# A scan kernel regrouped: from 128 tokens of one sequence per tile to 64 tokens of each of two sequences

## The chip, the cores and the metric

One core of one Trainium2 chip. The metric is device microseconds (us) of one execution; lower is better. The engines named below are PE (TensorE: matrix products; PEld is its weight load), DVE (VectorE), ACT (ScalarE), POOL (GpSimd, used here mostly to issue DMAs, those that add into their destination among them) and SP (SyncE, used only to issue DMAs).

## The reference

Two blocks, one after the other. The first is a gated linear recurrence per batch entry b (4) and head h (8), with 768 steps and a head size of 48:

```
scale = min(|a|, 0.999) / (|a| + 1e-6);   a = (a_re + i a_im) * scale
S_t   = diag(a_t) S_{t-1} + k_t v_t^T            (complex S, 48 x 48, real k and v)
y_t   = q_t^T Re(S_t)
```

The outputs y are laid out as 3072 tokens x 384 features (batch and step, head and head dimension), and the second block is a maxout network on them:

```
h   = max(x w1, x w2, x w3)        (384 -> 768)
out = h w_out                      (768 -> 384)
```

All inputs are float32 except the four weight matrices, which arrive as float64.

## The kernel before, in words

**Tiles and groups.** A tile x is 128 tokens of one sequence (all heads and features, 384 columns); a group g is the two tiles, x = 2g and x = 2g + 1 (written x and y in the schedule's words), of a pair of sequences. There are 12 groups: six steps of 128 tokens for sequences 0 and 1, then six for sequences 2 and 3 (`NS` = 6). Within a tile the recurrence is worked in two chunks of 64 tokens. A complex decay is a magnitude and an angle; products of decays become sums of logarithms and sums of angles.

**The steps of a group.** `gates` (L501) makes the logarithm of the magnitude (tile `Ln`) and the angle in turns (tile `w`) for both tiles at once. `angles` (L582) sums the angles over tokens: step `cs` multiplies a triangle of ones, `upto`, by `w` on PE; `t` (ACT) and `nf` (DVE) take off whole turns; `Cd` sends the last token's sum to the first token of the next group's angles, by a DMA of POOL's that adds into the tile `ar` of group g + 1. There it is added after step `half` (DVE) has made `ar` and before step `turn` (DVE) reads it. `turns` (L618) sums `Ln` by matrix products `sums` and `F`, takes exponentials on ACT, and multiplies k and q by them and by sine and cosine (`mk`, `mq`, `uk`, `uq`, `kEn` on DVE); `tp` transposes on PE, and `Kc` and `Qc` copy to SBUF on ACT or DVE. `factors` (L683) makes the scaled copies `Q1`, `Q2`, `KB`, `QB`, `QG` on DVE. `scores` (L714) makes the masked 64 x 64 score blocks from `A` and `B`.

**The state.** `state` (L766) keeps the states that a tile's two chunks start from in the buffers `g0` to `g3`. `dk` (PE) is the sum of k v^T of a chunk; `h0` to `h3` (L784) move the state on: `h0` multiplies by the first chunk's decay and `h1` adds its `dk`, which gives the state for the second chunk; `h2` and `h3` do the same for the second chunk, which gives the state for the next tile of the sequence. Each works on all heads of one chunk (384 elements a partition), on DVE, and on ACT where there is only `dk` to copy. The first step of a pair of sequences starts from zero, and the last one leaves out `h2`, `h3` and half of `dk`.

**Outputs.** `outputs` (L801), step `y`, adds the score product and, where there is a state, the product of `QG` with the state. The maxout block takes a group's 256 tokens at a time: `U` (PE, three weight blocks of 128 columns at a time) and `u` (the maximum), and for the second product seven half-size products `P1` to `P7` with sums `S1` to `S4`. Group 0 is done tile by tile with tiles xT and hT instead, while the weights are still being turned from float64 to float32 by steps `Wa` to `Wg` on ACT, DVE and POOL.

**What sets the order.** Nothing is scheduled at run time. `SCHEDULE` (L21) is a written list of words `step:group`; `run` (L954) issues each word's instructions, and `Bound` (L199) ties each engine to the order of issue, so every engine (and each DMA queue, SP's and POOL's) works through its own instructions strictly in that order. `SLOTS` (L124) names which of four pairs of PSUM banks each product uses. A word in `OTHER` (L131) goes to the second of two places: a load to POOL's queue and not SP's, a copy, an absolute value or a maximum to DVE and not ACT, an addition to DVE and not to a DMA of POOL's.

The products of `cs` are these: for each chunk and each half of the heads the weights are 128 tokens x 64, so that a chunk's sums run over all tokens of the tile up to its own.

```python
for ch in range(2):
    for j in range(2):
        dst, m = ps[j * L64:(j + 1) * L64, ch * HC:(ch + 1) * HC], slice(ch * L64, (ch + 1) * L64)
        mm(out=dst, lhsT=upto[:, m], rhs=every(T["w", g][:, c * DM:(c + 1) * DM], j), start=True, stop=True)
```

Of the kernel before, what the change touches and what calls it, by code (L numbers as in the profile page):

```python
# [26 lines left out]
mqx:0 Wa10:0 nfx:0 WL11:0 afx:0 csy:0 Wb10:0 ty:0 sqr:1 Wc9:0 Wc10:0 T2:0 nfy:0 sbx:0 sax:0 We9:0 ukx:0 Wf9:0 f1x:0
t2:0 f2x:0 We10:0 Lix:2 uqx:0 Lky:0 f2y:0 tpkx:0 kEnx:0 Wf10:0 f0x:0 sqi:1 Wa11:0 WL1:0 Wb11:0 add:1 sumsy:0 Eky:0
tpqx:0 CL:0 Qcx:0 Kcx:0 Wa1:0 Q2x:0 lnL:1 WL2:0 Q1x:0 Eqy:0 relu:1 Wb1:0 Wc11:0 T1:0 expe:1 Eny:0 Wc1:0 expw:1 abs:1
Lvx:0 Lry:2 t1:0 We11:0 dkx:0 h1x:0 xor:1 Ax:0 Wf11:0 Wa2:0 Lqy:0 lne:1 g0x:0 We1:0 Liy:2 g1x:0 Lkx:1 Wb2:0 QBx:0  # L30
half:1 g2x:0 Wc2:0 g3x:0 pw:1 Wf1:0 M0:0 afy:0 lnw:1 h2x:0 WL4:0 Lnop:1 expL:1 We2:0 Wa4:0 KBx:0 mulai:1 mulw:1 h3x:0
Cdy:0 Wb4:0 Bx:0 stt:1 Lrx:2 sqr:2 Wf2:0 say:0 sby:0 QGx:0 M1:0 b1x:0 atan:1 mqy:0 Wc4:0 uqy:0 Wg1:0 b0x:0 yx:0 Cdx:0
tpqy:0 sqi:2 add:2 xor:2 turn:1 lnL:2 Lvy:0 relu:2 Lqx:1 WL5:0 We4:0 xx:0 Qcy:0 mky:0 M2:0 Wf4:0 expe:2 Wa5:0 csx:1
uky:0 m0:0 m1:0 Q2y:0 Lqy:1 tpky:0 Fx:1 tx:1 Kcy:0 f0x:1 Q1y:0 nfx:1 csy:1 QBy:0 Ay:0 expw:2 Wg2:0 abs:2 kEny:0 Wg4:0
Wb5:0 WL7:0 U01x:0 ty:1 g0y:0 f1x:1 lne:2 nfy:1 dky:0 g1y:0 f2x:1 f3x:1 addw:2 Wa7:0 half:2 Cdx:1 u01x:0 U11x:0 Z2:0
g2y:0 Wc5:0 g3y:0 KBy:0 h1y:0 By:0 b1y:0 b0y:0 QGy:0 lnw:2 Cdy:1 We5:0 Wb7:0 Wf5:0 sumsx:1 h2y:0 u11x:0 expL:2 mulai:2
yy:0 xy:0 mulw:2 Eqx:1 Wc7:0 Ekx:1 Enx:1 U02x:0 h3y:0 afx:1 sax:1 stt:2 Wg5:0 afy:1 We7:0 U02y:0 U01y:0 U11y:0 WL8:0
u02x:0 atan:2 U12y:0 turn:2 sbx:1 Wf7:0 u01y:0 u02y:0 Lix:4 u11y:0 Fy:1 Wg7:0 sumsy:1 Wa8:0 Wb8:0 mkx:1 u12y:0 mqx:1
U21y:0 sby:1 f0y:1 Wc8:0 csx:2 Lnop:2 f1y:1 f3y:1 Lkx:2 f2y:1 Z4:0 Eky:1 csy:2 Eny:1 u21y:0 Eqy:1 uqx:1 ty:2 tpqx:1
Qcx:1 U21x:0 We8:0 ukx:1 tpkx:1 u21x:0 Lvx:2 Wf8:0 nfy:2 Kcx:1 tx:2 Z3:0 Wg8:0 Lky:1 kEnx:1 sumsx:2 nfx:2 Fx:2 U22y:0  # L40
h0x:1 u22y:0 Lvx:1 QBx:1 say:1 Lqy:2 dkx:1 Liy:3 mqy:1 Q1x:1 Enx:2 Q2x:1 mky:1 afx:2 sax:2 Lvy:2 KBx:1 h1x:1 sbx:2
h2x:1 Ekx:2 Eqx:2 uqy:1 afy:2 Oy:0 oy:0 Liy:4 tpqy:1 h3x:1 uky:1 QGx:1 Bx:1 Qcy:1 Ax:1 tpky:1 f1x:2 f0x:2 f2x:2 f3x:2
Q1y:1 Kcy:1 Lqx:2 g0x:1 Q2y:1 sby:2 say:2 U22x:0 g1x:1 g2x:1 g3x:1 mkx:2 Lrx:3 u22x:0 Lix:3 KBy:1 Lvy:1 sqi:3 b1x:1
Ay:1 sumsy:2 kEny:1 mqx:2 Lky:2 QBy:1 uqx:2 b0x:1 Eky:2 U12x:0 u12x:0 Eqy:2 yx:1 xx:1 ukx:2 Lry:3 tpqx:2 tpkx:2 Eny:2
g0y:1 Qcx:2 g1y:1 g2y:1 g3y:1 sqr:3 xor:3 add:3 lnL:3 relu:3 h0y:1 dky:1 By:1 Q1x:2 QGy:1 h1y:1 J3:0 h2y:1 Dy:0 Kcx:2
Q2x:2 Ox:0 b1y:1 mqy:2 b0y:1 ox:0 yy:1 mky:2 uky:2 xy:1 QGx:2 expe:3 Lqx:3 Ax:2 g0x:2 Lrx:4 expw:3 abs:3 half:3 addw:3
# [5 lines left out]
P4:1 h3y:2 expw:4 r1:1 abs:4 addw:4 g1y:2 g2y:2 lne:4 P6:1 xor:4 sax:3 QGy:2 g3y:2 Px:1 sby:3 P7:1 sbx:3 Dx:0 P3:1
mqx:3 r6:1 half:4 h0x:3 P2:1 By:2 r5:1 r7:1 r57:1 oy:1 lnw:4 sumsy:3 b1y:2 b0y:2 Fy:3 ukx:3 Cdx:3 Eny:3 uqx:3 Eky:3
expL:4 ox:1 Cdy:3 Eqy:3 f3y:3 Lvy:3 f0y:3 yy:2 xy:2 tpqx:3 mulai:4 tpkx:3 Qcx:3 mqy:3 Lnop:4 mulw:4 QBx:3 Q1x:3 Lky:3
say:3 stt:4 sqi:5 uqy:3 Lry:5 sqr:5 Kcx:3 KBx:3 mky:3 U01:2 Lvx:3 Q2x:3 U02:2 f2y:3 uky:3 add:5 f1y:3 Dx:1 u01:2 u02:2
# [87 lines left out]
def kernel(  # L143
# [15 lines left out]
    P = 128  # L159
# [882 lines left out]
```

## Time and profile before

| what | value |
|---|---|
| three runs | 566.14, 567.57, 568.57 us; median 567.57 |
| the profiled execution | 566.42 us, its span 564.7 us |
| mean granted TensorE clock | 0.978 |
| PE, DVE, ACT, POOL busy | 527.8, 490.0, 391.5, 153.5 us |
| HBM read, written | 33.03 MB, 4.72 MB |
| POOL's DMAs of step `Cd` (ar<-nf) | 40, median 3.1 us from issue to landing |

The page gives the busy time of each engine, the span in 40 equal slices of 14.1 us (a digit is the busy share in tenths; PEclk is the granted clock), the chain that ended last and the costliest groups of instructions. A busy time is the union of the instructions' intervals. Consecutive instructions of one engine overlap a little in these records, so the distance from one start to the next is shorter than a mean duration. The code is issued through one helper, so all work carries line L208, and the rows are told apart by their tiles (`out<-in`). Each float32 matrix product shows as two records.

### The profile page before, as it was taken

The numbers are of one execution on the slowest core, as the hardware profiler recorded it, in microseconds if no ns is written. First come the engines' busy times: TensorE is split into PE (matmuls) and PEld (weight loads), VectorE is DVE, ScalarE is ACT, GpSimd is POOL, SyncE is SP. The second block draws the span as 40 slices with busy tenths as digits, with TensorE's granted clock in tenths as the row PEclk, the third lists the DMA queues.
The fourth block names the chain that finished last, engine by engine and source line by source line (L and its number), as shares of the span: only waits on it lengthen the run. The fifth ranks groups of instructions, "written<-read, shape, count | busy, mean of one in ns | idle before, by whom it ended". The sixth has DMA issues, their size and how long they took to land.

```text
span 564.7 us, 22778 instructions
## 1 busy us (share of the span) xinstructions
PE 527.8 (93%) x10086; PEld 452.2 (80%) x10086; DVE 490.0 (87%) x777; ACT 391.5 (69%) x668; POOL 153.5 (27%) x243
## 2 busy tenths in 40 slices
PE   2568799999998999999999999999999999999997
PEld 1345597678887888988888888998888898988896
DVE  7999959999998999999999889999998868997324
ACT  7898868976888878998686897766668644641100
POOL 8615553304040030102605205215550181000000
PEclk9779989999999999999999999999999999999999
DMA  9995983514424244717307323525341132000000
GB/s 249 267 253 88 193 171 68 104 33 81 78 47 89 53 87 87 141 35 139 59 11 156 58 42 68 99 46 110 76 90 28 30 60 73 3 30 2 2 29 28
DMA packets 108916, 47.53 MB, mean 84 GB/s; under 512 B 95633, under 2 KB 100241, under 8 KB 108817
## 3 DMA queue, kind: packets, MB, share of 16 engines
q1 hardware_dynamic: 99136, 31.08, 24.9%
q0 software_dynamic: 9680, 14.99, 14.3%
q8 instruction: 79, 1.29, 0.9%
q14 instruction: 21, 0.16, 0.1%
HBM read 33.03 MB, written 4.72 MB: 67 GB/s over the span
## 4 chain that ended last, share of the span: by engine, by line
PE 75%; ACT 6%; DVE 2%; issue 1%; SPq 1%; DMA 1%; DVEq 0%; ACTq 0%
PE up L208 30%; PE op L208 21%; PE y L208 6%; PE A L208 4%; PE tp L208 4%; PE dk L208 3%; PE sums L208 2%; PE cs L208 2%; ACT L208 2%; PE F L208 1%; PE B L208 1%; SPq L208 1%; DMA ar<-in_a_re_dram 1%; DVE atm L208 1%; ACT f L208 1%
## 5 line engine op out<-in xcount | busy, mean ns | idle before, releaser
L208 PE MATMUL up<-xhx,w 128*128 128x256 f32 x792 | 177.7, 382 | 0.7 <-ACT K L208 0.4
L208 PEld LDWEIGHTS up<-xhx,w 128*128 128x128 f32 x792 | 148.4, 190 | 22.5 <-ACT K L208 0.6
L208 ACT ACT_TABLE_LOAD x59 | 75.7, 1283 | 1.7 <-PEq L1026 0.8
L208 POOL DMA_DIRECT2D ar<-nf x40 | 35.7, 1261 | 73.9 <-DVE ar L208 71.1
L208 PE MATMUL op<-wo,xhx 128*128 128x192 f32 (+1 forms) x220 | 49.1, 363 | 0.1
L208 DVE TENSOR_TENSOR Q<-Q,f 112x1024 f32<-112x1024 f32 (+1 forms) x48 | 44.8, 951 | 0.7 <-ACT Q L208 0.7
L208 POOL DMA_DIRECT2D k<-in_k_dram x52 | 36.7, 1021 | 30.1 <-DVE uk L208 29.6
L208 DVE TENSOR_TENSOR ot<-ot,op 128x192 f32<-128x192 f32 (+1 forms) x66 | 27.2, 417 | 19.0 <-PE op L208 11.5
L208 POOL DMA_DIRECT2D w<-L x7 | 6.2, 884 | 130.9 <-ACT L L208 65.4
L208 POOL DMA_DIRECT2D vb<-in_v_dram x48 | 34.1, 967 | 27.5 <-PE y L208 27.5
L208 ACT ACTIVATE f<-F 48x232 f32<-48x232 f32 x96 | 34.2, 359 | 10.5 <-PE F L208 8.4
L208 PEld LDWEIGHTS op<-wo,xhx 128*128 128x128 f32 x220 | 36.7, 190 | 4.3 <-issue 0.6
L208 ACT COPY atm<-B 32x128 f32<-32x128 f32 x96 | 24.6, 256 | 21.9 <-DVE atm L208 14.2
L208 PE MATMUL y<-atm,vb 128*32 128x64 f32 x1152 | 38.5, 221 | 0.7 <-POOL uk L208 0.5
L208 PE MATMUL y<-QG,g 112*32 112x64 f32 x1408 | 37.5, 219 | 0.0
L208 PEld LDWEIGHTS y<-atm,vb 128*32 128x32 f32 x1152 | 31.9, 109 | 6.7 <-issue 2.9
L208 PEld LDWEIGHTS y<-QG,g 112*32 112x32 f32 x1408 | 34.5, 109 | 0.0
L208 PE MATMUL op<-wo,strassen 128*128 128x192 f32 x176 | 33.0, 331 | 0.0
L208 PE MATMUL A<-Q,K 112*32 112x80 f32 x1536 | 31.5, 234 | 1.4 <-issue 1.3
L208 PE MATMUL op<-w,strassen 128*128 128x192 f32 x176 | 32.3, 328 | 0.0
L208 DVE COPY_PREDICATED atm<-masko,A 128x256 f32<-128x256 uint8 x72 | 30.8, 433 | 1.4
L208 ACT COPY ot<-op 128x192 f32<-128x192 f32 (+1 forms) x13 | 4.4, 342 | 38.0 <-PE op L208 37.9
(155 smaller groups left out, 1205.8 us busy)
## 6 DMA issues: line engine op xcount, KB each, us to landing
ai<-in_a_im_dram SPq DMA_DIRECT2D x24, 192.0 KB, 4.3
ar<-in_a_re_dram SPq DMA_DIRECT2D x24, 192.0 KB, 3.4
out_dram<-ot SPq DMA_DIRECT2D x24, 192.0 KB, 2.2
Ln<-e POOLq DMA_DIRECT2D x10, 384.0 KB, 4.5
q<-in_q_dram SPq DMA_DIRECT2D x60, 48.0 KB, 2.8
w<-L POOLq DMA_DIRECT2D x7, 384.0 KB, 4.4
k<-in_k_dram POOLq DMA_DIRECT2D x52, 48.0 KB, 4.0
w<-in_moe_w_dram SPq DMA_DIRECT2D x3, 768.0 KB, 6.4
```

The costliest lines, as they stand in the source:

```text
L208: ins = f(*a, **kw)
```

## The change

A tile is now 64 tokens of each of two sequences, and a group is the same 64 tokens of all four. The two chunks of a tile belong to two sequences and don't depend on each other; one chain of 12 steps takes the place of two chains of six. What follows from it:

- `rows` and `half` (in place of `halves`) index by sequence; `load_a` issues two DMAs of 64 partitions where it issued one of 128.
- `cs` uses 64 x 64 triangles, each chunk in its own PSUM bank and with its own 64 tokens alone.
- `Cd` sends the last sum of every sequence: four DMAs a tile where there were two, and for 11 groups where there were 10.
- `h0` and `h1` alone are left; each works on both chunks (768 a partition).
- Group 0 alone starts from zero (without `h0`, `QG` and the products of `y` with `g`), and group 11 has no `dk` and no `h`.
- The output's DMA writes 64 rows of two sequences.
- `SCHEDULE`, `SLOTS` and `OTHER` are written anew from end to end. Counted over the program: DVE has 779 instructions before and 731 after (`g` operations 80 -> 40, `K` and `Q` copies 9 -> 7, `L<-ar` 5 -> 3, `xhx<-y` 6 -> 5, `af` 7 -> 6, `QG` 24 -> 22), ACT 670 and 676 (table loads 59 -> 61, the copies and absolute values that DVE lost, `g` copies 4 -> 2), POOL 248 and 300 (`ar<-nf` 40 -> 88, loads 136 -> 140, `w<-L` 7 -> 8, `w<-w` 4 -> 3), SP 238 and 282, and PE 5438 in both.

```diff
-Liy:0 sqi1:0 Zg:0 Zf:0 Lry:0 sqr1:0 Lix:0 add1:0 lnL1:0 sqi0:0 Lrx:0 sqr0:0 add0:0 expw1:0 WL0:0 WL3:0 expe1:0 relu1:0
+Lry:0 sqr1:0 Liy:0 sqi1:0 add1:0 xor1:0 Lix:0 Lrx:0 lnL1:0 expe1:0 Zg:0 WL0:0 Zf:0 Lkx:0 expw1:0 lne1:0 relu1:0
...
     TG = C * P
-    NS = S // P
-    NG = B // C * NS
+    NG = S // L64
     NX = NG * C
     HU = 4
 
...
         dims = [list(d) for d in view.ap]
         return bass.AP(view.tensor, view.offset, dims[:-1] + [[P - D, 2], [1, D]])
 
-    def rows(a, g, c):
-        b, s = divmod(g, NS)
-        return a[b * C + c, :, s * P:(s + 1) * P, :].rearrange("h t d -> t h d")
-
-    def halves(a, g, c, j):
-
-        b, s = divmod(g, NS)
-        return a[b * C + c, j::2, s * P:(s + 1) * P, :].rearrange("h (c t) d -> t c h d", c=2)
+    def rows(a, g, b):
+
+        return a[b, :, g * L64:(g + 1) * L64, :].rearrange("h t d -> t h d")
+
+    def half(a, g, b, j):
+
+        return a[b, j::2, g * L64:(g + 1) * L64, :].rearrange("h t d -> t h d")
 
     def load_a(g, c, nm, src):
         t = once((nm, g), lambda: ld2.tile([P, C, H, D], FP, tag=nm, name=nm))
-        sp.dma_start(out=t[:, c], in_=rows(src, g, c))
+        for ch in range(2):
+            sp.dma_start(out=t[ch * L64:(ch + 1) * L64, c], in_=rows(src, g, 2 * c + ch))
 
     def load_kq(g, c, nm, src):
         t = T[nm, g * C + c] = ldx.tile([P, 2, 4, D], FP, tag=nm, name=nm)
         for j in range(2):
             for ch in range(2):
-                (pool if other() else sp).dma_start(out=t[j * L64:(j + 1) * L64, ch], in_=halves(src, g, c, j)[:, ch])
+                (pool if other() else sp).dma_start(out=t[j * L64:(j + 1) * L64, ch], in_=half(src, g, 2 * c + ch, j))
 
     def load_v(g, c):
         x = g * C + c
...
         for j in range(2):
             for ch in range(2):
                 (pool if other() else sp).dma_start(out=T["v", x][j * L64:(j + 1) * L64, ch, :, j * D:(j + 1) * D],
-                                                    in_=halves(v, g, c, j)[:, ch])
+                                                    in_=half(v, g, 2 * c + ch, j))
 
     def every(view, j):
 
...
             dve.scalar_tensor_tensor(out=w, in0=w, scalar=-1.0 / math.pi, in1=ar, op0=OP.mult, op1=OP.add)
         return True
 
+    def chunked(t):
+        return t.rearrange("p (c n) -> p c n", c=2)
+
     def angles(g, c, name):
 
         x = g * C + c
         if name == "cs":
-            ps = T["cs", x] = banks("cs", DM)
-            for ch in range(2):
-                for j in range(2):
-                    dst, m = ps[j * L64:(j + 1) * L64, ch * HC:(ch + 1) * HC], slice(ch * L64, (ch + 1) * L64)
-                    mm(out=dst, lhsT=upto[:, m], rhs=every(T["w", g][:, c * DM:(c + 1) * DM], j), start=True, stop=True)
+            ps = T["cs", x] = banks("cs")[:, :, 0:HC]
+            for j in range(2):
+                for ch in range(2):
+                    r = slice(ch * L64, (ch + 1) * L64)
+                    mm(out=ps[j * L64:(j + 1) * L64, ch], lhsT=upto[r, r],
+                       rhs=every(T["w", g][r, c * DM:(c + 1) * DM], j), start=True, stop=True)
         elif name == "t":
             T["t", x] = nat2.tile([P, DM], FP, tag="t", name="t")
-            activation(out=T["t", x], in_=T["cs", x], func=AF.Copy, scale=-1.0, bias=MAGIC)
+            activation(out=chunked(T["t", x]), in_=T["cs", x], func=AF.Copy, scale=-1.0, bias=MAGIC)
         elif name == "nf":
             T["nf", x] = nat2.tile([P, DM], FP, tag="nf", name="nf")
-            dve.scalar_tensor_tensor(out=T["nf", x], in0=T["t", x], scalar=MAGIC, in1=T["cs", x],
+            dve.scalar_tensor_tensor(out=chunked(T["nf", x]), in0=chunked(T["t", x]), scalar=MAGIC, in1=T["cs", x],
                                      op0=OP.subtract, op1=OP.add)
         elif name == "Cd":
-            if (g + 1) % NS > 0:
-                t = flat(T["ar", g + 1])[0:1]
-                for j in range(2):
-                    last = (j + 1) * L64
-                    pool.dma_start(out=every(t[:, c * DM:(c + 1) * DM], j), accum_op=OP.add,
-                                   in_=T["nf", x][last - 1:last, HC:].rearrange("p (i d) -> p i d", d=D))
+            t = flat(T["ar", g + 1])[:, c * DM:(c + 1) * DM]
+            for j in range(2):
+                for ch in range(2):
+                    last, first = (j + 1) * L64, ch * L64
+                    pool.dma_start(out=every(t[first:first + 1], j), accum_op=OP.add,
+                                   in_=T["nf", x][last - 1:last, ch * HC:(ch + 1) * HC].rearrange("p (i d) -> p i d", d=D))
         elif name == "af":
             T["af", x] = nat2.tile([P, DM], FP, tag="t", name="af")
             magnitude(T["af", x], T["nf", x])
...
 
     def factors(x, name):
 
-        def times(out, in_, c, n, g=0):
-
-            f = T["F", x][0:DD].rearrange("p s j n -> p (s j) n")[:, g:, c:c + n]
+        def times(out, in_, c, n):
+
+            f = T["F", x][0:DD].rearrange("p s j n -> p (s j) n")[:, :, c:c + n]
             f = f.rearrange("p g (n e) -> p g n e", e=1)
-            dve.tensor_tensor(out=out, in0=in_, in1=f.to_broadcast([DD, 2 * H - g, n, 8]), op=OP.mult)
+            dve.tensor_tensor(out=out, in0=in_, in1=f.to_broadcast([DD, 2 * H, n, 8]), op=OP.mult)
 
         if name in ("Q1", "Q2"):
             Q = T["Q", x][0:DD]
...
             times(rows8(QB[0:DD]), rows8(T["Q", x][0:DD].rearrange("p (g j) t -> p g j t", j=2)[:, :, 1, 0:32]), C32, 4)
         elif name == "QG":
             QG = T["QG", x] = un1.tile([P, 2 * H, L64], FP, tag="QG", name="QG")
-            g = 0 if x // C % NS > 0 else H
-            times(rows8(QG[0:DD, g:]), rows8(T["Q", x][0:DD, 2 * g:, 0:32]), CG, 8, g)
+            times(rows8(QG[0:DD]), rows8(T["Q", x][0:DD, :, 0:32]), CG, 8)
         else:
             return False
         return True
...
 
     def state(x, name):
 
-        s = x // C % NS
-        G = T["G", x] = gs[x % 4]
-
-        def four(t):
-
-            return heads(t).rearrange("p i j d -> p j i d")
+        def both_chunks(t):
+
+            return heads(t.rearrange("p c i n -> p (c i) n"))
 
         if name == "dk":
             ps = T["dk", x] = banks("dk")
-            for n in range(H if s < NS - 1 else 4):
+            for n in range(H):
                 ch, i = divmod(n, 4)
                 for j in range(2):
                     r = slice(j * L64, (j + 1) * L64)
                     for lo, hi in ((0, L64), (L64, DD)):
                         mm(out=ps[lo:hi, j, n * D:(n + 1) * D], lhsT=both(T["Uk", x], n)[r, lo:hi],
                            rhs=T["v", x][r, ch, i, j * D:(j + 1) * D], start=True, stop=True)
-        elif name[0] == "h" and name[1:].isdigit():
-            c, i = divmod(int(name[1:]), 2)
-            new = four(G[0:DD, 1] if c == 0 else gs[(x + C) % 4][0:DD, 0])
-            dk = T["dk", x][0:DD, :, 0:DM].rearrange("p j (c i d) -> p c j i d", c=2, d=D) if i else None
-            if c > 0 and s == NS - 1 or s + c + i == 0:
+        elif name in ("h0", "h1"):
+            new = both_chunks(gs[(x + C) % 4][0:DD])
+            if name == "h0":
+                F = T["F", x][0:DD, :, :, CD:CD + 1]
+                dve.tensor_tensor(out=new, in0=both_chunks(gs[x % 4][0:DD]), in1=F.to_broadcast([DD, H, 2, D]), op=OP.mult)
                 return True
-            if i == 0:
-                F = T["F", x][0:DD, :, :, CD:CD + 1].rearrange("p (c i) j n -> p c j i n", c=2)
-                dve.tensor_tensor(out=new, in0=four(G[0:DD, c]), in1=F[:, c].to_broadcast([DD, 2, 4, D]), op=OP.mult)
-            elif s + c == 0:
-                act.copy(out=new, in_=dk[:, c])
+            dk = T["dk", x][0:DD, :, 0:DM].rearrange("p j (n d) -> p n j d", d=D)
+            if x < C:
+                act.copy(out=new, in_=dk)
             else:
-                dve.tensor_tensor(out=new, in0=new, in1=dk[:, c], op=OP.add)
+                dve.tensor_tensor(out=new, in0=new, in1=dk, op=OP.add)
         else:
             return False
         return True
...
 
         g, c_ = divmod(x, C)
         if name == "y":
-            atm, V, G, QG = T["atm", x], T["v", x], gs[x % 4], T["QG", x]
+            atm, V, G, QG = T["atm", x], T["v", x], gs[x % 4], T.get(("QG", x))
             y = T["y", x] = banks("y", DM).rearrange("p (k t) -> p k t", k=KD)
             queues = [[] for _ in range(4)]
             for r in range(DM // 32):
...
                 for c in range(2):
                     k_ = r // 4 if g == 0 else (r // 4 + 2 * (g % 2)) % KD
                     todo = [(V[:, c, i, 32 * w:32 * w + 32], atm[:, 4 * c + i])]
-                    for n in ((0,), (1, 2), (3,))[w] if x // C % NS > 0 or c > 0 else ():
+                    for n in ((0,), (1, 2), (3,))[w] if g > 0 else ():
                         todo.append((G[0:DD, c, i, 32 * n:32 * n + 32], QG[0:DD, 2 * (4 * c + i) + n // 2]))
                     queues[r % 4] += [(r, c, k_, l, m, n == 0, n == len(todo) - 1) for n, (l, m) in enumerate(todo)]
             for n in range(max(map(len, queues))):
...
             T["ot", x] = fp2.tile([P, DM], FP, tag="ot", name="ot")
             act.copy(out=T["ot", x], in_=T["op", x])
         elif name == "D":
-            t0 = x // C // NS * C * S + x % C * S + x // C % NS * P
-            sp.dma_start(out=out[t0:t0 + P, :], in_=T["ot", x])
+            g, c = divmod(x, C)
+            sp.dma_start(out=out.rearrange("(b s) m -> b s m", s=S)[2 * c:2 * c + 2, g * L64:(g + 1) * L64], in_=T["ot", x])
         else:
             return False
         return True
```

More of the change, by code (lines that the diff above doesn't have):

```diff
@@ L27 @@
[L27 to L46, printed above, removed]
@@ L52 @@
[L52 to L55, printed above, removed]
-tpqy:3 Lqx:4 tpky:3 atan:4 Kcy:3 Ax:3 lnL:5 S3:2 Qcy:3 Liy:6 Bx:3 g0x:3 g1x:3 g2x:3 kEnx:3 Lkx:4 U11:2 turn:4 g3x:3
@@ new lines @@
+ty:0 mqx:0 afx:0 Lix:2 sax:0 t2:0 sqr:1 sumsy:0 Wc10:0 f1y:0 Wf9:0 Lqy:0 uqx:0 tpqx:0 Qcx:0 add:1 Wa11:0 lnL:1 ukx:0
+tpkx:0 We10:0 Kcx:0 Q2x:0 Q1x:0 relu:1 xor:1 expe:1 Wb11:0 nfy:0 Lry:2 afy:0 Wf10:0 Lqx:1 Ax:0 Wc11:0 T0:0 kEnx:0
+expw:1 abs:1 Eky:0 We11:0 pw:1 WL2:0 g0x:0 WL1:0 half:1 Wf11:0 g1x:0 Lrx:2 Lvx:0 t0:0 Wa1:0 Wb1:0 g2x:0 Wc1:0 Wa2:0
+Cdy:0 g3x:0 Eqy:0 Eny:0 lne:1 lnw:1 We1:0 expL:1 Wb2:0 M0:0 say:0 Lnop:1 mqy:0 Wf1:0 WL4:0 sby:0 sqr:2 Cdx:0 Wc2:0
+dkx:0 mulw:1 mulai:1 uqy:0 sqi:2 tpqy:0 We2:0 stt:1 Wa4:0 Wf2:0 Lix:4 Qcy:0 add:2 Wg1:0 atan:1 Wb4:0 turn:1 h1x:0
```

183 lines of the change are left out of this document (101 added, 82 removed).

## Prediction

> **What bounds the kernel now.** I read the page's busy times and slices first, then the chain that ended last, then the windows.
>
> ```profile
> PE 527.8 (93%) x10086; PEld 452.2 (80%) x10086; DVE 490.0 (87%) x777; ACT 391.5 (69%) x668; POOL 153.5 (27%) x243
> ...
> PE   2568799999998999999999999999999999999997
> ...
> PEclk9779989999999999999999999999999999999999
> ...
> PE 75%; ACT 6%; DVE 2%; issue 1%; SPq 1%; DMA 1%; DVEq 0%; ACTq 0%
> ```
>
> PE is busy 93% of the span, and in the row of slices every slice from the sixth on (70 us) shows a 9, but for one 8 and a 7 at the very end. The chain of work is PE for 75%. So there are two regimes, and the windows (per row: the stretch, its length, then busy time of PE, PE's weight loads, DVE, ACT and POOL, the granted clock, DMA share and GB/s) give their sizes.
>
> ```profile
> 20.00:40.00 20.00, 13.03 (x210) 9.66 (x210) 20.00 (x33) 18.66 (x30) 5.72 (x10) 0.66 1.10 249
> ...
> 60.00:80.00 20.00, 15.35 (x355) 12.76 (x354) 13.07 (x23) 13.14 (x26) 12.30 (x16) 0.83 0.87 173
> ...
> 200.00:250.00 50.00, 49.94 (x938) 44.28 (x932) 48.31 (x77) 42.81 (x70) 6.21 (x7) 1.00 0.50 92
> ```
>
> In the first 80 us PE is busy 52.3 us and idle 27.7, at a granted clock of 0.66 to 1.0, while DVE is busy 68.8 and ACT 65.1: weight conversion and the first two groups' gates lead there. From 80 to 540 us PE idles only 5.6 us in all; after that, 3.6 us are lost at the tail. In this second regime an operation taken from PE shortens the kernel by its whole duration, unless something else becomes late. DVE is that candidate: 48.31 of 50 us in the last row shown.
>
> **The angle sums, step `cs`.** A tile has 4 products, 8 records. The PE timeline shows start and duration of merged runs of records:
>
> ```profile
> 357.29 1.52 PE L208 MATMUL cs<-w,upto 128*64 128x192 f32 x16
> 358.74 1.08 PE L208 MATMUL dk<-vb,uk 64*64 64x48 f32 x62
> ...
> 426.12 0.56 PE L208 MATMUL sums<-Ln,rest 64*64 64x192 f32 x8
> 426.45 0.56 PE L208 MATMUL sums<-Ln,mid 64*64 64x192 f32 x8
> ```
>
> Before, the 16 records of a group's two tiles start at 357.29 and the next work at 358.74: 1.45 us a group, 0.725 a tile. After, a product is 64 x 64 weights with 192 columns, four of them covering both row and both column halves of the array, in the same loop order as `sums` and, as there, into two banks. So the row that prices it is `sums`, of equal shape: 8 records from 426.12 to 426.45, 0.33 us; behind other work the first eight take 0.37. I take 0.35. A tile saves 0.375 us. Ten groups (2 to 11) lie in the PE-bound regime: 20 tiles, **-7.5 us**. The lower bound comes from the mean busy times of the groups (20.3 us for 192 records of `cs`, 14.0 for 192 of `sums` with `mid`): 6.3 us by 20/24 is 5.3. The upper bound takes the slowest `cs` at full clock (0.81 a tile) against 0.33: 9.6. Groups 0 and 1 are counted at nothing here, since PE is waiting around them. Reading the two banks costs nothing new: `E<-sums` reads the same shape in 489 ns a time, `t<-cs` now in 489 too.
>
> **The state.** The DVE timeline gives the distance of starts:
>
> ```profile
> 342.58 0.95 DVE L208 TENSOR_TENSOR w<-w,L 128x768 f32<-128x768 f32 x1
> 343.44 0.55 DVE L208 TENSOR_TENSOR g<-g,f 112x384 f32<-112x384 f32 x1
> 343.91 0.55 DVE L208 TENSOR_SCALAR ar<-ar 128x768 int32<-128x768 int32 x1
> 344.38 0.94 DVE L208 TENSOR_TENSOR xhx<-xhx,up 128x768 f32<-128x768 f32 x1
> ```
>
> 384 elements take 0.47 us (343.44 to 343.91), 768 take 0.86 (342.58 to 343.44). 80 operations at 0.47 become 40 at 0.86 or 0.87: 37.6 to 34.8, 2.8 us less. With the copies and absolute values that the new list gives to ACT, and summing such distances over both programs, DVE's work falls from 474.9 to 468.0 us, 6.9 less. ACT gains two table loads at 1.28, two `K` and `Q` copies at 1.0, two `L<-ar` at 0.84, one `af` and one `xhx<-y` at 0.5, and loses 0.2: 7 us more on 391.5. From group 2 on I price this at **0**, hidden under PE, which ends last; if PE's lead over DVE is not there, it is the first rival below.
>
> **The start.** Group 0 loses its four state operations (4 x 0.47) and its two half-size `QG` (2 x 0.6, 112x512 from start to start): 3.1 us less DVE work, most of which lies ahead of the first `up` products, and DVE leads there (39.7 of 40 us from 20 to 60). Group 1's `turn` and the last weight blocks stand 4 to 5 us earlier in DVE's new order by those sums, but PE's and ACT's orders changed too. I take **-2 us**, with -5 (all of that) and +3 as ends; +3 is what PE's shorter waits of this stretch (1.8 to 2.7 us each) cost one at a time.
>
> **Loads and output.** The 96 halves of `ar` and `ai` carry the same bytes. SP spends 0.57 us on an issue, 48 more make 27 us on a queue that waits 160 us for `ot` alone; the first tile's data come one issue later: 0 to +0.6, taken as **0**. The output's DMA keeps its size.
>
> **The carry, step `Cd`.** POOL issues 88 of these DMAs where it issued 40. Four now carry one tile, eight a group, and `turn` of the next group must wait for the last to land. POOL's timeline:
>
> ```profile
> 344.75 3.19 POOL L208 DMA_DIRECT2D ar<-nf  x4 [30.05 <-DVE ar L208]
> 346.80 3.71 POOL L208 DMA_DIRECT2D vb<-in_v_dram  x4
> ```
>
> `half` starts at 343.91 (above) and lasts 0.55, the first `Cd` begins 0.3 us after its end, and four take 2.05 us of the queue (344.75 to 346.80), 0.51 each. Landing takes 3.1 us from the issue. Eight therefore need 0.3 + 7 x 0.51 + 3.1 = 7.0 us behind `half`. In the changed DVE order I summed the distances between the later of `nf` and `half` and the next `turn`, for the 11 groups: 12.1, 15.6, 12.4, 11.7, 11.8, 11.6, 23.9, 10.1, 7.4, 14.3, 19.9 us. All exceed 7.0, the ninth by 0.4. Behind the eight in POOL's queue stand an `Ln<-e`, a `w<-L` or loads, later by 2 us; they aren't needed within that. So **0**, with the other end in the slower rival.
>
> [...] Here single `Cd`s do vary from 778 to 2060 ns. [...]
>
> **Sum.** The profiled execution is 566.42 us, 1.7 more than its span. 566.4 - 7.5 - 2 = 556.9. The median of the three runs stands 1.15 above that execution, so the forecast is **558.0 us**, 1.7% less. A difference under 0.5% (2.8 us) can't be told from none here. Its own range, from -9.6 - 5 to -5.3 + 0, is 553 to 562.
>
> **Rivals.**
> 1. *DVE takes over as the bound.* PE would wait for DVE from group 2 on, and only DVE's own saving counts. That is 6.9 less 3.1 spent in the start, 3.8 us, and no gain at the start: 562.6, as a median **563.8**. For it: DVE is busy 90 to 97% in every stretch of 50 us from 100 to 400. Against it: over that stretch it still idles more than PE does.
> 2. *The new order gives the gain back.* The orders of all five engines are new, and PE's waits in the start are single ones of up to 9.8 us (`F`, for `Ln`). One more of that size cancels everything: 566.4 - 9.5 + 9.8, as a median **567.9**. With it goes the case that the products don't run four at a time, so that the change doesn't do what it says: 566.4 - 2, as a median 565.6. `sums` speaks against that.
> 3. *Slower: the carry is late.* If each of the eight takes 1.5 us of the queue (between the mean duration of 1.26 and the longest of 2.06), they need 0.3 + 7 x 1.5 + 3.1 = 13.9 us, and seven of the eleven gaps fall short, by 20.2 us in sum. DVE stands at `turn` for that long, and behind it stands all that PE waits for: 566.4 - 9.5 + 20.2, as a median **578.2**. It comes out slower by over 0.5% from 1.34 us an issue on, where the shortfalls pass 12.3 us. For it: twice the DMAs in one burst. Against it: 0.51 measured in a burst of four.
>
> **How the numbers follow.** Chances: forecast 0.55, DVE as bound 0.17, gain given back 0.14, late carry 0.14. Leaving out the late carry and the upper part of the second rival, the range is 551 (2 us under the forecast's own low end, for an order that also shortens PE's waits after 80 us) to 568. Faster by over 0.5% means under 564.7: the forecast and nearly all of the first rival, 0.71; within 0.5%: the second rival and a rest, 0.14; slower: the third and a little of the second, 0.15.
>
> **What would show it.** In the profile of the changed kernel `cs` should stand as 64*64 with about 0.7 us from a group's first record to the next work, PE busy near 519 us, and `g` as 40 rows of about 950 ns. PE's idle time in the first 80 us should be near 26 us, and between 80 and 530 stay under 8. If DVE's waits name DMA `ar<-nf`, or PE waits for DVE `w` ahead of `cs`, the third rival is at work; if PE's waits name DVE rows evenly, the first. The forecast is wrong if PE's busy time doesn't fall, or if its idle time grows by what was saved.

## The result, and the profile after

Four runs of the changed kernel have a median of 585.29 us (581.5 to 587.46), against 567.08 us for four of the kernel before; the ratio is 1.031 (95% interval 1.025 to 1.037). It is 3.1% **slower**, where 558.0 us (1.7% less) was forecast with a range of 551 to 568. The profiled execution took 587.46 us, its span 585.8. In this kernel the helper's line is L206.

The page's busy times, the slices of PE, the granted clock and the chain:

```profile
PE 530.7 (91%) x10086; PEld 451.2 (77%) x10086; DVE 483.9 (83%) x729; ACT 395.8 (68%) x674; POOL 193.5 (33%) x295
...
PE   2568989998999999999999998997999999999973
...
PEclk9998999999999999999999998997999999999997
...
PE 55%; DMA 13%; ACT 10%; issue 7%; DVE 6%; SPq 4%; POOL 4%; DVEq 0%; ACTq 0%; POOLq 0%
```

The chain has changed its nature: PE's share falls from 75% to 55%, and DMA, 1% before, holds 13%. Of 40 slices of 14.6 us, the 25th and the 28th (from 351 and 395 us) now show 8 and 7 for PE, the clock dips with them, and the last two show 7 and 3. The windows for two stretches that the prediction reads and for two where PE lost time (columns as there):

```profile
60.00:80.00 20.00, 17.42 (x365) 12.81 (x368) 18.42 (x29) 16.23 (x34) 13.32 (x18) 0.99 0.69 161
...
200.00:250.00 50.00, 49.35 (x1019) 43.43 (x1018) 46.85 (x72) 38.89 (x68) 29.32 (x42) 1.00 0.43 80
...
350.00:450.00 100.00, 93.94 (x1745) 81.74 (x1736) 80.80 (x120) 67.16 (x118) 28.02 (x40) 0.95 0.28 54
...
540.00:590.00 50.00, 32.57 (x262) 29.04 (x260) 11.31 (x21) 1.93 (x4) 0.00 (x0) 0.88 0.05 16
```

The row of before for the third stretch:

```profile
350.00:450.00 100.00, 99.09 (x2110) 87.98 (x2109) 92.76 (x145) 69.68 (x125) 29.69 (x45) 1.00 0.33 67
```

From 350 to 450 us PE idles 6.1 us (0.9 before) and behind 540 us 13.2 of the 45.8 that are left (3.6 before).

PE's waits are not the whole loss. From 100 us on it has four waits of over 2 us: 2.1 at 144 us, 2.7 at 353, 2.6 at 400 and 4.0 at 569. Behind each of them the granted clock is lower: 0.66 from 145 to 150 us, 0.77 from 355 to 360, 0.66 from 400 to 410, 0.77 from 570 to 575. There the products themselves take longer, as these rows of `up` alone show (busy time and records of PE, granted clock, DMA share and GB/s):

```profile
400.00:410.00 10.00, 6.75 (x18) 0.66 0.48 82
430.00:440.00 10.00, 7.72 (x37) 1.00 0.11 38
```

A record of `up` lasts 379 ns in the middle at full clock (200 to 250 us) and 634 behind the wait at 400 us. The work itself does what the diff says. First PE's timeline, then DVE's groups:

```profile
175.51 0.88 PE L206 MATMUL cs<-w,upto 64*64 64x192 f32 x16
176.32 1.99 PE L206 MATMUL up<-xhx,w 128*128 128x256 f32 x8
```

```profile
L206 DVE TENSOR_TENSOR g<-g,f 112x768 f32<-112x768 f32 x20 | 19.0, 950 | 0.0
L206 DVE TENSOR_TENSOR g<-g,dk 112x768 f32<-112x768 f32 x20 | 19.0, 949 | 4.9 <-PE dk L206 4.8
```

A group's `cs` takes 0.81 us from its start to the next work, where it took 1.45, and the state's 40 operations take 950 ns each. So the loss is elsewhere. The timeline of the tail names it:

```profile
562.48 15.32 SPq L206 DMA_DIRECT2D out_dram<-ot  x4
...
569.07 0.32 ACT L206 COPY ot<-op 128x192 f32<-128x192 f32 x1 [15.76 <-DMA out_dram<-ot]
...
569.44 2.93 PE L206 MATMUL op<-w,strassen 128*128 128x192 f32 x8 [4.01 <-ACT ot L206]
...
573.01 1.40 DVE L206 TENSOR_TENSOR ot<-ot,op 128x192 f32<-128x192 f32 x3 [7.50 <-DMA out_dram<-ot]
...
576.72 0.55 DVE L206 TENSOR_TENSOR ot<-ot,op 128x384 f32<-128x384 f32 x1 [0.56 <-PE op L206]
```

ACT and DVE want one of the two `ot` buffers for the last group, and the output DMAs of the group before still hold them; PE waits for ACT. The last operation ends at 577.27 and the span at 585.8: from there the last output DMA takes 8.5 us, where it took 3.0 before. These 5.5 us and the 4.0 that PE waits for ACT are nearly all of the 9.6 us by which PE idles longer at the tail. The chain has one of these DMAs by itself:

```profile
560.27 0.97 DVE xhx L206
563.05 9.85 DMA out_dram<-ot
573.81 2.88 PE op L206 x16
```

In mid-kernel a second kind of wait stands, here at 342 us:

```profile
342.42 0.95 POOL L206 DMA_DIRECT2D w<-L  x1
...
342.45 0.56 SPq L206 DMA_DIRECT2D out_dram<-ot  x1
...
350.08 0.84 ACT L206 ACTIVATE L<-w 128x768 f32<-128x768 f32 x1 [7.07 <-DMA w<-L]
...
352.10 0.96 DVE L206 TENSOR_TENSOR w<-w,L 128x768 f32<-128x768 f32 x1 [3.09 <-ACT L L206]
...
353.25 4.98 PE L206 MATMUL up<-xhx,w 128*128 128x256 f32 x14 [2.70 <-ACT E L206]
```

The adding DMA `w<-L` of POOL's and an output DMA of SP's are issued at the same moment. ACT, which waits for `w<-L`, goes on 7.7 us after the issue, and behind ACT DVE waits 3.09 us and PE 2.70.

### The profile page after: what moved, and what is told of

Its sections match the earlier page's. It is cut to its first block, busy times and chain, and to the rows that moved or that the text cites. A ratio compares the mean times of both kernels' runs of the same rounds, so it can differ in the third digit from the quotient of the medians.

```text
span 585.8 us, 22902 instructions
## 1 busy us (share of the span) xinstructions
PE 530.7 (91%) x10086; PEld 451.2 (77%) x10086; DVE 483.9 (83%) x729; ACT 395.8 (68%) x674; POOL 193.5 (33%) x295
## 3 DMA queue, kind: packets, MB, share of 16 engines
q0 software_dynamic: 11088, 15.23, 14.6%
## 4 chain that ended last, share of the span: by engine, by line
PE 55%; DMA 13%; ACT 10%; issue 7%; DVE 6%; SPq 4%; POOL 4%; DVEq 0%; ACTq 0%; POOLq 0%
PE up L206 21%; PE op L206 17%; SPq L206 4%; PE y L206 4%; PE tp L206 3%; DMA ar<-in_a_re_dram 3%; DMA w<-L 3%; PE A L206 2%; ACT L206 2%; DMA xhx<-in_moe_w_out_dram 2%; POOL ar L206 2%; PE dk L206 2%; DMA ai<-in_a_im_dram 2%; DMA out_dram<-ot 2%; ACT f L206 1%
## 5 line engine op out<-in xcount | busy, mean ns | idle before, releaser
L206 PE MATMUL up<-xhx,w 128*128 128x256 f32 x792 | 184.1, 391 | 3.2 <-ACT E L206 3.2
L206 PEld LDWEIGHTS up<-xhx,w 128*128 128x128 f32 x792 | 152.2, 195 | 28.0 <-ACT E L206 3.5
L206 POOL DMA_DIRECT2D ar<-nf x88 | 73.3, 1647 | 54.2 <-DVE ar L206 44.9
L206 POOL DMA_DIRECT2D k<-in_k_dram x56 | 38.7, 871 | 60.1 <-DVE uk L206 49.6
L206 PE MATMUL op<-wo,xhx 128*128 128x192 f32 (+1 forms) x220 | 48.8, 363 | 0.4 <-ACT K L206 0.4
L206 POOL DMA_DIRECT2D q<-in_q_dram x48 | 36.2, 1138 | 35.1 <-DVE uq L206 33.4
L206 DVE TENSOR_TENSOR xhx<-xhx,up 128x768 f32<-128x768 f32 x22 | 20.9, 952 | 31.0 <-PE up L206 30.5
L206 DVE TENSOR_TENSOR Q<-Q,f 112x1024 f32<-112x1024 f32 (+1 forms) x48 | 45.0, 951 | 1.7 <-ACT f L206 1.5
L206 ACT ACTIVATE f<-F 48x232 f32<-48x232 f32 x96 | 34.2, 359 | 13.2 <-PE F L206 9.6
L206 PE MATMUL y<-atm,vb 128*32 128x64 f32 x1152 | 38.9, 221 | 2.5 <-ACT atm L206 2.4
L206 DVE TENSOR_TENSOR ot<-ot,op 128x192 f32<-128x192 f32 (+1 forms) x66 | 27.0, 417 | 16.3 <-DMA out_dram<-ot 7.5
L206 ACT ACTIVATE xhx<-up 128x768 f32<-128x768 f32 x18 | 14.6, 810 | 38.2 <-PE up L206 38.0
L206 PEld LDWEIGHTS op<-wo,xhx 128*128 128x128 f32 x220 | 36.6, 190 | 4.5 <-ACT K L206 0.5
L206 ACT COPY atm<-B 32x128 f32<-32x128 f32 x96 | 24.6, 256 | 22.2 <-PE B L206 10.8
L206 PE MATMUL op<-w,strassen 128*128 128x192 f32 x176 | 34.2, 341 | 4.8 <-ACT ot L206 4.3
L206 PEld LDWEIGHTS y<-atm,vb 128*32 128x32 f32 x1152 | 32.5, 109 | 6.9 <-issue 3.7
L206 PE MATMUL y<-QG,g 112*32 112x64 f32 x1408 | 36.7, 219 | 0.0
L206 PE MATMUL A<-Q,K 112*32 112x80 f32 x1536 | 31.9, 239 | 4.8 <-ACT En L206 2.8
L206 PEld LDWEIGHTS op<-w,strassen 128*128 128x128 f32 x176 | 29.9, 196 | 6.8 <-ACT ot L206 5.1
L206 PEld LDWEIGHTS y<-QG,g 112*32 112x32 f32 x1408 | 34.3, 109 | 0.0
L206 POOL DMA_DIRECT2D w<-L x8 | 7.2, 894 | 82.1 <-ACT L L206 44.4
```

What stands on the lines that cost most here:

```text
L206: ins = f(*a, **kw)
```

## The experiments

Theory **D**: the form of the output's DMA, now 2 x 64 rows x 384, makes it slow, and it slows others. Theory **O**: the new order as a whole. Theory **C**: the carry. Every ratio is to the kernel before, timed beside it on the same chip, with its 95% interval; 0.001 is 0.57 us. In the code, `...` stands for lines left out.

**1. Outputs split.**

```diff
-sp.dma_start(out=out.rearrange("(b s) m -> b s m", s=S)[2 * c:2 * c + 2, g * L64:(g + 1) * L64], in_=T["ot", x])
+for ch in range(2):
+    sp.dma_start(out=out.rearrange("(b s) m -> b s m", s=S)[2 * c + ch, g * L64:(g + 1) * L64],
+                 in_=T["ot", x][ch * L64:(ch + 1) * L64])
```

> The changed kernel with each output DMA (2 x 64 rows x 384) given as two, one a sequence, 64 rows each; 48 issues where there were 24. Theory D, that the form of the output's DMA is what is slow (9.85 us for its landing at the end against a median of 2.2 before): the last one lands in 2 to 4 us, the waits for out_dram<-ot at the end (15.8 us of ACT, 7.5 of DVE) go, and 8 to 12 us go from the tail; if the waits of ACT for w<-L and for loads (7.1, 4.1, 4.4, 3.5 us) come from the same DMAs, up to 9 more: 585.3 becomes 565 to 577. Theory O, that the new order is what is slow and the outputs merely come late: within 2 us of 585. Theory C (the third rival, the carry's DMAs): within 2 us of 585 too.

Measured: 565.18 us, 0.995 (0.992 to 0.998). The same bytes in twice as many DMAs take about 20.7 us off the changed kernel (1.031 to 0.995); it is now a little faster than before. The span ends 3.6 us behind the last operation and PE's wait for `ot` at the tail is 0.3 us where it was 4.0. ACT still stands 12.0 us for `out_dram<-ot` there, against 15.8: so most of that wait cost nothing. From 100 us on no wait of PE's is over 0.9 us, and the granted clock is 1.00 from 100 to 563 us. Between the two profiled executions PE's idle time falls by 12.4 us and its busy time by 7.1. The DMA list of this run against that of the changed kernel (number, KB, median us to landing):

```profile
out_dram<-ot SPq DMA_DIRECT2D x48, 96.0 KB, 2.5
```

```profile
out_dram<-ot SPq DMA_DIRECT2D x24, 192.0 KB
```

In the changed kernel the landing is blank, and so it is in the rows of SP's loads. The list of before has 2.2 us for the output. The rows are blank again in the kernel before with outputs of 2 and of 4 blocks, and not with 16 (experiment 3), so here a blank stands with the forms that cost (1.031, 1.018 and 1.006, against 1.002 for 16).

**2. Only the last two groups' outputs split**, groups 0 to 9 as in the changed kernel.

```diff
...
+if g < 10:
+    sp.dma_start(out=seqs[2 * c:2 * c + 2, g * L64:(g + 1) * L64], in_=T["ot", x])
+for ch in range(2) if g >= 10 else ():
+    sp.dma_start(out=seqs[2 * c + ch, g * L64:(g + 1) * L64], in_=T["ot", x][ch * L64:(ch + 1) * L64])
```

> The changed kernel with the output DMAs of groups 10 and 11 alone given as two; those of groups 0 to 9 keep their form. Theory D by the tail alone: 8 to 12 us less than 585.3, and nothing between this and the version with all of them split. Theory D with the body (outputs of groups 0 to 9 slow the DMAs that ACT waits for): 8 to 12 us less here, and the version with all split is another 4 to 9 us below this one. Theories O and C: within 2 us of 585.

Measured: 1.013 (1.006 to 1.019). So some 10.6 us (1.031 to 1.013) are the tail's, and another 10.1 (1.013 to 0.995) come from groups 0 to 9, each give or take 4 to 5 by the intervals: those outputs delay what other engines wait for. Here ACT still waits 8.50 us for `w<-L` at 348 us and 4.41 for a load at 397; with all outputs split these are 5.24 and none, and the median landing of `w<-L` is 5.6 us against 6.8 in the changed kernel and 7.2 here. `w<-L` is in POOL's queue, so this is not SP's queue alone.

**3. The kernel before with this form of DMA**, and with 4 and 16 blocks.

```diff
...
-sp.dma_start(out=out[t0:t0 + P, :], in_=T["ot", x])
+g, c = divmod(x, C)
+p, s = divmod(g, NS)
+t0 = s * P + c * L64
+sp.dma_start(out=out.rearrange("(b s) m -> b s m", s=S)[C * p:C * p + 2, t0:t0 + L64], in_=T["ot", x])
```

> The kernel before, each output DMA writing 64 rows of each of the pair's two sequences (the second half of a tile goes to another place, so the rows of the output are permuted); bytes and number of DMAs unchanged. Theory D: the last landing takes about 10 us and not 2.2 to 4.7, and the ot buffers are held longer: 567.1 becomes 573 to 582. Theories O and C: 566 to 569.

```diff
...
-sp.dma_start(out=out[t0:t0 + P, :], in_=T["ot", x])
+n = P // 16
+sp.dma_start(out=out.rearrange("(r s) m -> r s m", r=16)[:, x * n:(x + 1) * n], in_=T["ot", x])
```

> The kernel before, each output DMA writing 16 blocks of 8 rows to 16 places of the output (rows permuted), same bytes and number. [...] Rival, that writing to several places at all is slow: like the form with two blocks, 1.015 to 1.025.

For the third, 4 stands in place of 16.

> The same with 4 blocks of 32 rows to 4 places. [...] Rival: 1.015 to 1.025.

Measured: 2 blocks 1.018 (1.012 to 1.024), 4 blocks 1.006 (1.004 to 1.009), 16 blocks 1.002 (0.999 to 1.004). Writing to several places costs nothing that shows by itself (at most 0.4%, by the interval of 16); few outer blocks do (1.8% with 2, 0.6% with 4). Both 4 and 16 lie under the rival's 1.015. From the end of the last `ot` operation to the end of the span it is 9.05 us with 2, 5.70 with 4, 3.63 with 16, and 3.02 for one run of 128 rows. Fitted to the first and third of these, 2.8 us plus 12.5 us divided by the number of blocks gives 9.05 and 3.6, and 5.9 for 4. Each is one execution; in the changed kernel and in its version with half the carry (experiment 4) the same distance is 8.5.

The delay in the other queue shows here as well, with everything else in its old order. First the row of before, then with 2 blocks:

```profile
w<-L POOLq DMA_DIRECT2D x7, 384.0 KB, 4.4
```

```profile
w<-L POOLq DMA_DIRECT2D x7, 384.0 KB, 6.2
```

With 4 blocks it is 5.4 us, with 16 blocks 4.0. Why few blocks take longer, no run here shows.

**4. The carry.** First on the changed kernel as it is, then on the version with split outputs.

```diff
-for ch in range(2):
+for ch in range(1):
     last, first = (j + 1) * L64, ch * L64
```

> The changed kernel with the carry of the first sequence of each tile alone, so two of its DMAs a tile and not four (the second sequence's angles lose their carry). Theory C: POOL's queue is shorter by 4 x 0.5 us a group and w<-L or Ln<-e, which wait behind, land earlier; 5 to 15 us less than 585.3. Theories D and O: within 1.5 us of 585.3.

> The changed kernel with its output DMAs split, and with the carry of the first sequence of each tile alone (44 of its DMAs where there are 88; the second sequence's angles lose their carry). To be held against the split version's ratio of 0.995 to the kernel before. Theory C1, that the longer carry takes what is still missing from the forecast (loads of q and w<-L wait behind it in POOL's queue, turn waits 1.95 us once): 2 to 5 us less, ratio 0.986 to 0.991. Theory P, that what is missing is PE's own work (products that were priced too high, and waits at other places): ratio 0.993 to 0.997.

Measured: 1.024 (1.018 to 1.030) on the changed kernel, which can't be told from its 1.031 (1.025 to 1.037); 0.985 (0.982 to 0.988) with split outputs, 5.7 us under the split version. So the carry does cost once the outputs are split. Whether it cost in the changed kernel itself, where the middles of the two intervals lie 4 us apart, stays open. Without any carry, to see if that goes on:

```diff
 elif name == "Cd":
-    t = flat(T["ar", g + 1])[:, c * DM:(c + 1) * DM]
...
+    pass
```

> The changed kernel with its output DMAs split and no carry at all (no DMA of step Cd; every group's angles lack it). If the carry costs in proportion to its DMAs, 88 fewer than the split version give another 5 us below the halved carry: ratio 0.975 to 0.980. If only the last of eight comes too late and four come early enough: as the halved carry, 0.982 to 0.987.

Measured: 0.988 (0.985 to 0.991). No gain beyond the halved carry: it isn't a price per DMA. What is left is that a few come too late. The same bytes in half as many DMAs, one reading both halves of the source row and writing to partitions 0 and 64:

```diff
...
+src = T["nf", x][last - 1:last].rearrange("p (c i d) -> p c i d", c=2, d=D)
+to = every(t[0:1], j)
+dims = [list(d) for d in to.ap]
+to = bass.AP(to.tensor, to.offset, [[dims[0][0] * L64, 2]] + dims[1:])
+pool.dma_start(out=to, accum_op=OP.add, in_=src)
```

> The changed kernel with its output DMAs split, and with the carry's two DMAs of a tile and half of the heads (one a sequence) given as one that reads both halves of the source row and writes to two partitions: 44 DMAs where there were 88, same bytes, nothing left out. If the carry costs by the number of its DMAs, this gets all that the halved carry got: ratio 0.983 to 0.988 to the kernel before. If it costs by what the DMAs carry and where they land: 0.992 to 0.997, like the split version.

Measured: 561.13 us, 0.989 (0.986 to 0.993), with nothing left out: the fastest version that does all of the work. It is just above what the halved carry would give (0.983 to 0.988), and its interval touches that of the split version (0.992 to 0.998). POOL's and DVE's timelines for the same group, first split, then merged:

```profile
355.02 6.45 POOL L206 DMA_DIRECT2D ar<-nf  x8 [12.30 <-DVE ar L206]
...
364.09 0.96 DVE L206 SCALAR_TENSOR_TENSOR w<-w,ar 128x768 f32<-128x768 f32 x1 [1.95 <-DMA ar<-nf]
```

```profile
349.19 3.49 POOL L206 DMA_DIRECT2D ar<-nf  x4 [11.80 <-DVE ar L206]
...
356.23 0.95 DVE L206 SCALAR_TENSOR_TENSOR w<-w,ar 128x768 f32<-128x768 f32 x1
```

`turn` (w<-w,ar) starts 9.1 us behind the first of eight and has waited 1.95 for the last; behind four it waits for nothing. In the split version DVE also waits 2.91 us at 326.6 for a load of q that stands behind the previous carry in POOL's queue.

Which of the two paths counts, the landing or the queue? DMAs that add into a spare tile hold the queue, and nobody waits for them:

```diff
...
 to = every(t[first:first + 1], j)
+if ch == 1:
+    to = spare[2 * x + j:2 * x + j + 1].rearrange("p (i d) -> p i d", d=D)
```

> The changed kernel with its output DMAs split; the second sequence's carry DMAs are still issued at the same places, but add into a spare tile that nobody reads (its angles lose their carry). If the carry costs through POOL's queue (loads, Ln<-e and w<-L issued later, or POOL slower beside DVE): ratio 0.992 to 0.997, like the split version. If it costs because turn waits for the last of eight to land: 0.983 to 0.988, like the halved carry.

Measured: 0.991 (0.987 to 0.995), between the two expectations, and the interval reaches into both. With a spare DMA behind each real one:

```diff
-pool.dma_start(out=every(t[first:first + 1], j), accum_op=OP.add,
+for to in (every(t[first:first + 1], j), spare[n:n + 1].rearrange("p (i d) -> p i d", d=D)):
+    pool.dma_start(out=to, accum_op=OP.add,
...
```

> The changed kernel with its output DMAs split; each carry DMA is followed by one of the same source and size that adds into a spare tile: 176 in POOL's queue, the output right. If a DMA in POOL's queue costs whether or not somebody waits for it: some 8 to 12 us above the split version, ratio 1.008 to 1.018. If the cost is only that the last real one lands later: the eighth real one is issued 7 x 0.5 to 0.8 us later, so turn waits up to 5 us a group where the gap is short, and the loads behind come late too; the two are told apart here by the waits that the trace names (turn for ar<-nf against ACT and DVE for loads and w<-L).

Measured: 1.055 (1.053 to 1.058), far over the expected 1.018. Both paths show: `turn` waits 16.6 us in five waits for `ar<-nf`, and a load of q costs DVE 7.3 us. In the kernel before, the same edit and the carry given in twice as many:

> The kernel before, each carry DMA followed by one of the same source and size that adds into a spare tile: 80 in POOL's queue where there were 40, the output right. If a DMA in POOL's queue costs by itself: like the carry given in twice as many, 1.010 to 1.016. If it costs by the wait of turn for the landing: a tenth to a half of that, 1.001 to 1.007, since only one real DMA a tile comes later by one slot.

```diff
+for i in (0, 2):
+    pool.dma_start(out=every(t[:, c * DM:(c + 1) * DM], j)[:, i:i + 2], accum_op=OP.add,
...
```

> The kernel before with each of the carry's DMAs given as two of half the heads: 80 where there were 40, same bytes, same order. Theory C1: turn or the loads behind the carry in POOL's queue come late, 2 to 5 us more, ratio 1.004 to 1.009. The forecast's zero: ratio 0.998 to 1.002.

Measured: 1.005 (1.003 to 1.007) with the extra ones, 1.013 (1.009 to 1.016) with the real ones in twice as many, more than the 1.009 expected; its `turn` waits 3.43 us for the landing at 217 us. Forty more DMAs in POOL's queue cost 2.7 us there, and 7.3 if the work waits for them. Taking the loads off POOL's queue instead, in the merged version:

```diff
-Lky:0 abs1:0 Lqx:0 Lkx:0 Lvy:0 Lqy:0 Lqx:1 Wg4:0 Wg7:0 Wg8:0 Lvy:2 Lvx:1 Lky:1 Lkx:2 Lqx:3 Lqy:3 Lky:4 Lky:3 Lvx:4
+abs1:0 Wg4:0 Wg7:0 Wg8:0
...
```

(and so on through `OTHER`, all words Lk, Lq and Lv)

> The version with the carry merged (44 DMAs) and the output split, and all 35 load steps of k, q and v that POOL issues moved to SP's queue. If what is left of the carry's cost is loads that wait behind it: 1 to 4 us less than the merged version's 0.989, so 0.982 to 0.987. If not, or if SP's queue, which stands behind the output and freed buffers, brings them later: 0.988 to 1.000.

Measured: 1.022 (1.020 to 1.025). That is outside both ranges, and on the side of the second: from 254.5 us on SP issues 20 load DMAs and four outputs without a pause, a load of k comes behind them at 273.8, and at 278.7 DVE has waited 6.98 us for it. So this told nothing of the carry.

**5. The angle sums, and the state.** The first kernel takes the change's own edit of `cs`, `t` and `nf` into the kernel before; the second undoes it in the split version, by the diff below.

> The kernel before with the angle sums alone changed: 64 x 64 weights into two banks (the second chunk loses the first chunk's sums). All else, the order too, stays. Forecast's term: 7.5 us less, by the measured distances 6.4: ratio 0.987 to 0.989. If DVE takes over as the bound (the first rival): 3 us less or none, ratio 0.994 to 1.000.

> The changed kernel with its output DMAs split, and the angle sums with 128 x 64 weights as before (a chunk's sums then also take in the other sequence's tokens, which they shouldn't). By the forecast's term the new sums are worth 7.5 us; by the distances in the changed kernel's trace (1.45 to 0.81 us a group, ten groups) 6.4. Where PE is the bound, this kernel is slower than the split one by that: ratio 1.006 to 1.009 to the kernel before. If PE's time is no longer what ends last (waits hide it): 0.995 to 1.000.

```diff
-r = slice(ch * L64, (ch + 1) * L64)
-mm(out=ps[j * L64:(j + 1) * L64, ch], lhsT=upto[r, r],
-   rhs=every(T["w", g][r, c * DM:(c + 1) * DM], j), start=True, stop=True)
+m = slice(ch * L64, (ch + 1) * L64)
+mm(out=ps[j * L64:(j + 1) * L64, ch], lhsT=upto[:, m],
+   rhs=every(T["w", g][:, c * DM:(c + 1) * DM], j), start=True, stop=True)
```

Measured: 0.998 (0.996 to 1.000) for the new sums in the kernel before, so 1.1 us (0 to 2.2) and not 6 to 7.5; 1.003 (1.001 to 1.005) for the old sums in the split version, 4.6 us over its 0.995 and between the two expectations. In the first, the page says:

```profile
PE 521.3 (92%) x10086; PEld 444.6 (78%) x10086; DVE 490.1 (87%) x777; ACT 390.7 (69%) x668; POOL 154.1 (27%) x243
```

PE's busy time falls by 6.5 us and its idle time rises by 8.4 (36.9 to 45.3), 6.9 of them between 80 and 540 us (5.6 to 12.5): PE is done sooner and then waits. No single wait does it. The two largest for DVE behind `F`'s (`up` 4.2 us, `tp` for `uk` 4.1) stand in the kernel before too, with 4.2 and 3.6; what is new is spread over many waits for DVE and ACT of which the longest is 1.2 us (`dk` for `atm`, at 395 us). In the merged version, the sums undone by the same diff, and the state by the next one:

> The version with split outputs and merged carry, with the angle sums from 128 x 64 weights as before (sums then take in the other sequence's tokens). Forecast's term: 7.5 us more than the merged version, by the measured distances 6.4: ratio 0.999 to 1.004. If other engines share the bound, as in the order of before where the new sums gave 1 us: 0.989 to 0.994.

> The version with split outputs and merged carry, with each of the state's DVE operations of 768 elements a partition given as two of 384 (80 where there are 40), result unchanged. Forecast's price: nothing on the path, DVE 2.8 us more: ratio 0.986 to 0.992, like the merged version's 0.989. If DVE ends last: 2 to 3 us more, 0.992 to 0.996.

```diff
...
+for r in (slice(0, 4), slice(4, 8)):
+    if name == "h0":
+        dve.tensor_tensor(out=new[:, r], in0=old[:, r], in1=F[:, r], op=OP.mult)
+    else:
+        dve.tensor_tensor(out=new[:, r], in0=new[:, r], in1=dk[:, r], op=OP.add)
```

Measured: 1.003 (1.000 to 1.005) with the old sums, so they are worth 1.3%, 7.5 us (about 5 to 10) here; 0.988 (0.985 to 0.992) with the state in halves, no difference from 0.989.

By the middles of the intervals the steps add up. With split outputs, merged carry and the old sums the new order is at 1.003; the new sums take 1.3% off, the longer carry puts 0.5% on and the form of the output 3.6%, which gives 1.031.

## Why the prediction was wrong

- **Loads and output: the failed step.** "The output's DMA keeps its size" is true, and priced at 0. Its form was not looked at: with a destination of 2 blocks the span ends 8.5 us behind the last operation instead of 3.0, and one such DMA stands in the chain with 9.85 us. Experiment 1 puts the whole at about 20.7 us; by experiment 2 half of it is in the tail, through the last landing and the two `ot` buffers, and half in mid-kernel. There the traces show `w<-L` and a load late, PE waiting behind them, and products at a lower clock behind these waits. The diff showed the new slice, `[2 * c:2 * c + 2, ...]`; no rival had it.
- **The carry**: 0 forecast, 3 to 6 us measured with split outputs (0.995 against 0.985 to 0.989). The working took 0.51 us an issue, the distance of starts. But these DMAs start before the ones ahead are done: eight last 6.45 us, 0.81 each. With 0.81 the same working gives 9.1 us and not 7.0 (the trace: 9.4 from the end of `half` to `turn`), and the ninth gap, 7.4, falls short by 1.7, where DVE waits 1.95. So the third rival's mechanism was real, far below the 1.34 us from which it decides. In the changed kernel itself no wait names `ar<-nf`. How the rest divides between landing and queue stays open: the spare tile's interval holds both.
- **The angle sums**: -7.5 forecast, 7.5 (about 5 to 10) measured in the merged version, where PE's busy time is 520.3 us, 7.5 less than before. By the trace it is 0.64 us a group, 6.4 in all. The term was right, but the premise above it, that what is taken from PE shortens the kernel by its whole duration from 80 us on, is false in the old order, where it gave 1.1 us. A PE that is 93% busy had DVE and ACT close behind, and it waits for them in many small pieces. Why it held in the new order is open: giving DVE the state's operations in halves again changed nothing there.
- **The state**: 0 forecast, 0 measured.
- **The start**: -2 us forecast, not seen. PE's idle time in the first 80 us is 27.9 us in the changed kernel and 28.2 in the merged version, where 26 was to show it and 27.7 stood before. With split outputs, merged carry and the old sums, what is left of the change (start, state and order) is at 1.003 (1.000 to 1.005), 0 to 3 us slower than before and not 2 faster.
- **The signs**: PE's idle time from 80 to 530 us is 13.9 us where under 8 was asked for, and PE's busy time is 530.7 where 519 was. Part of that is work at a lower granted clock behind the new waits (0.95 from 350 to 450 us, 0.88 behind 540): `up` takes 184.1 us where it took 177.7, and 178.3 once the outputs are split.
- **The durations of `Cd`**, 778 to 2060 ns in the kernel before: in the bursts looked at they follow the place, as in the kernel with the spare tile:

```profile
349.78 0.83 POOL L206 DMA_DIRECT2D ar<-nf  x1 [11.99 <-DVE ar L206]
350.33 1.10 POOL L206 DMA_DIRECT2D spare<-nf  x1
350.83 1.42 POOL L206 DMA_DIRECT2D ar<-nf  x1
```

and so on to 2.88 us for the eighth; the bursts at 231, 394 and 433 us give 2.88 for it too.

## What to carry to other kernels

When a change turns one run of rows into blocks at several places, read how many outer blocks the DMA's destination has and not only its bytes: here two outer blocks made the last landing about three times as long (9.05 us against 3.02 in the kernel before), and giving the output as two DMAs brought 20.7 us back. Four waits of 2.1 to 4.0 us on PE cost more than their length in the changed kernel: behind them the granted clock was 0.66 to 0.77, and `up` took 184.1 us where it took 177.7. Price a burst of DMAs by when they end, not by the distance of their starts (0.81 us apart against 0.52 here), and hold it against the shortest gap. An engine that is 93% busy isn't proof that its work is what ends last: a short experiment on that one term in the old order shows 1 us for the 7.5.

## What was not expected of the hardware

- The last output of 196,608 bytes costs about 2.8 us plus 12.5 us divided by the number of outer blocks (2, 4, 16) in the kernel before, as worked out above. Two blocks also delay adding DMAs of another queue: `w<-L` lands in 6.8 us and not 5.6 in the new order, in 6.2 and not 4.4 in the old.
- POOL's adding DMAs of 768 bytes start 0.52 us apart and end 0.81 us apart, so the eighth of a burst lasts 2.88 us where the first lasts 0.83. In a burst of sixteen, with a spare DMA behind each real one, the fourteenth lasts 4.65, and the fifteenth starts only 2.4 us behind it.
- In the changed kernel each of PE's four waits of 2.1 to 4.0 us from 100 us on has a stretch at a granted clock of 0.66 to 0.77 behind it; in the split version, with no wait over 0.9 us, the clock is 1.00 from 100 to 563 us. No run here tells from what length on that begins.
